# A fused layer norm, attention and SwiGLU kernel: the last reciprocals read out of PSUM ahead of the copies for a flag, and the fallback's DMAs issued by GpSimd

## The chip, the cores and the metric

The kernel runs on one core of a Trainium2 chip. The metric is the device time of one execution in microseconds (us). Where a profile is quoted, its *span* is the time from the first to the last instruction of that execution; the device time is 1.8 to 2.0 us longer in most runs.

## The reference

```python
xn = layernorm(x)                           # x: 1 x 2048 x 512, bf16
s  = attention(xn, wq, wk, wv) @ wo         # 32 heads of 16; one k and one v head for all
g  = silu((silu(xn @ w_gate) * (xn @ w_up)) @ w_down)
return x + s * g
```

## The kernel before

A scheduler in the kernel lays some 20,000 instructions on the engines for the first 764 us. It takes the softmax without subtracting a maximum. That is right as long as the denominators are in range, so at the end a flag is computed from them; if it is raised, a fallback recomputes everything exactly. For the inputs here it is not raised, and every engine jumps over the fallback. The change touches the end of the kernel alone:

```python
    def tq_norm(half, qqs, src):          # src: transposed outputs in PSUM, denominators among them
        ...
        return [nc.vector.tensor_copy(out=dl[:, half, q0:q1, :, :], in_=t4[:, :, :, d0:d0 + 1]),
                nc.vector.reciprocal(out=rd[:, half, q0:q1, :, :], in_=dl[:, half, q0:q1, :, :]),
                nc.vector.tensor_tensor(out=o_tok[...], in0=t4[:, :, :, v0:v0 + DH], in1=rd[...], op=ALU.mult)]
    ...
    tq01, tq23 = ring[lb][:, 0:512], o_ps[:]
    tp = [ring[la][:, 512:1024], ring[lb][:, 512:1024]]
    ...
    for h, src in ((0, tq01), (1, tq23)):
        qqs = (2 * h, 2 * h + 1)
        tadd("DVE", tq_norm(1, qqs, src))
        tb = tp[h].bitcast(BF16)
        tadd("PE", [nc.tensor.transpose(out=tb[:, k * P:(k + 1) * P], in_=o_tok[:, qq, :], identity=ident_bf[:])
                    for k, qq in enumerate(qqs)])
        tadd("ACT", nc.scalar.copy(out=oTl[:, NQ - 1, h * H2:(h + 1) * H2], in_=tb[:, 0:2 * P]))
    dlf = dl[:].rearrange("p h q g o -> p (h q g o)")
    tadd("DVE", nc.vector.tensor_scalar(out=dlc[:], in0=dlf, scalar1=DEN_LO, scalar2=DEN_HI, op0=ALU.max, op1=ALU.min))
    ...                                    # three more small operations: all in range? -> fmin
    ...                                    # last projection matmuls; flag matmul between tiles 1 and 2
    tadd("DVE", e_out_mul(LN, obk[0], dsts[0]))
    ...                                    # flag_i; its loads on all engines; multiplies and adds of four tiles
    for k in range(4):
        tadd("SP", e_out_st(LN + k))       # the four last stores, 128 KB each
    MAIN.close()
    with tc.If(flag > 0):
        _exact_max_path(...)               # the fallback; its DMAs are issued by nc.sync
```

`tadd` keeps the order on each engine.

## Time and profile before

| | before |
|---|---|
| device time, 4 runs | median 780.86 us, 780.45 to 781.15 |
| span of the profiled run | 778.8 us |
| busy: TensorE, VectorE, ScalarE | 96%, 94%, 97% |
| VectorE's last add (L695) ends | 773.44 us |
| last store: end of issue, 15th of its 16 parts landed, 16th | 774.18, 775.65, 776.07 us |
| SyncE: end of its branch, next instruction | 774.27, 776.87 us |

The busy shares tell about the first 764 us, the rows below about the end, where the change is. The landings are the trace's updates of the store's semaphore: sixteen for one store. The prediction shows the lines of the profile that these readings rest on.

### The profile page before, as it was taken

What the parts mean: (1) busy time and instruction counts of PE and PEld (TensorE: products, weight loads), DVE (VectorE), ACT (ScalarE), POOL (GpSimd) and SP (SyncE); (2) the same over time, 40 slices, a digit from 0 to 9 for tenths busy, and PEclk for the clock granted to TensorE, in tenths of its full rate; (3) what the DMA queues carried; (4) which work ended last, traced back from release to release, by engine and by line L of the source; (5) the groups of instructions that cost most, each with busy time, mean ns of one, the idle gap of its engine ahead of it and who ended that gap; (6) DMA issues with size and microseconds to landing.
All of it is one profiled execution on the core that took longest, in us unless ns stands there. A gap on an engine that the chain in (4) does not pass through costs nothing.

```text
span 778.8 us, 20698 instructions
## 1 busy us (share of the span) xinstructions
PE 748.9 (96%) x9093; PEld 229.7 (29%) x9095; DVE 734.0 (94%) x920; ACT 756.9 (97%) x866; POOL 54.2 (7%) x59
## 2 busy tenths in 40 slices
PE   8999999999999999999999999999999999999995
PEld 3323223322222333322233322322223233322221
DVE  7689999999999999999999999999999999999995
ACT  6999999999999999999999999999999999999993
POOL 2100000000012000000001110000000300000101
PEclk9999999999999999999999999999999999999998
DMA  9400000000001000000000100000000000000001
GB/s 327 141 9 9 16 2 24 3 8 17 4 28 50 23 2 6 18 2 24 2 10 22 49 24 2 24 1 9 16 2 24 28 23 2 2 23 3 22 2 32
DMA packets 21193, 20.15 MB, mean 26 GB/s; under 512 B 8744, under 2 KB 17192, under 8 KB 21096
## 3 DMA queue, kind: packets, MB, share of 16 engines
q1 hardware_dynamic: 19512, 18.20, 7.7%
q8 instruction: 73, 1.20, 0.6%
q10 hardware_dynamic: 1584, 0.56, 0.3%
q14 instruction: 24, 0.20, 0.1%
HBM read 14.19 MB, written 2.34 MB: 21 GB/s over the span
## 4 chain that ended last, share of the span: by engine, by line
PE 48%; ACT 45%; DVE 5%; issue 1%; SPq 0%; DMA 0%; ACTq 0%; POOL 0%; DVEq 0%; POOLq 0%
ACT Pb L937 41%; PE ring L877 17%; PE m_ps L488 16%; PE o_ps L747 13%; ACT th L657 3%; DVE Bf L997 1%; ACT g_sb L937 1%; PE ring L433 1%; DVE Bf L1016 1%; ACT th L674 1%; DVE x_sb L997 0%; DVE Bf L1023 0%; PE ring L488 0%; DVE x_sb L1016 0%; PE ring L452 0%
## 5 line engine op out<-in xcount | busy, mean ns | idle before, releaser
L937 ACT ACTIVATE Pb<-ring 128x1024 bf16<-128x1024 f32 x772 | 730.7, 1202 | 2.1 <-PE ring L877 2.1
L877 PE MATMUL ring<-QB,KT 32*128 32x512 bf16 x2048 | 306.0, 382 | 15.6 <-ACT Pb L937 9.3
L997 DVE TENSOR_SCALAR Bf<-ring 128x1024 uint16<-128x1024 f32 x172 | 209.2, 1216 | 5.2 <-PE ring L877 3.7
L877 PEld LDWEIGHTS <-KT 32*128 32x128 bf16 x2048 | 94.1, 90 | 313.9 <-issue 307.4
L747 PE MATMUL o_ps<-Pb,VA 128*32 128x512 bf16 x1544 | 146.9, 385 | 0.0
L997 DVE TENSOR_SCALAR x_sb<-ring 128x1024 uint16<-128x1024 f32 x72 | 87.6, 1217 | 2.7 <-PE ring L877 2.4
L1016 DVE TENSOR_TENSOR Bf<-Bf,Bf 128x2048 f16<-128x2048 f16 x74 | 90.0, 1216 | 0.1
L747 PE MATMUL o_ps<-xnT,zw 128*32 128x512 bf16 x1092 | 83.1, 381 | 0.0
L488 PE MATMUL m_ps<-xnT,wu_sb 128*32 128x512 bf16 x896 | 72.6, 384 | 1.1 <-DVE ab L659 1.1
L488 PE MATMUL m_ps<-wd_sb,hT 128*32 128x512 bf16 x896 | 71.5, 383 | 0.1
L488 PE MATMUL m_ps<-xnT,wg_sb 128*32 128x512 bf16 x896 | 70.4, 384 | 0.0
L747 PE MATMUL o_ps<-Bf,VD 128*32 128x512 f16 x688 | 67.1, 385 | 0.4 <-DVE Bf L1016 0.3
L732 POOL TENSOR_TENSOR oT<-oa,rb 128x512 bf16<-128x512 f32 x15 | 22.7, 1514 | 614.2 <-DMA rb<-dscr 515.7
L1023 DVE TENSOR_SCALAR Bf<-Bf 128x2048 uint16<-128x2048 uint16 x86 | 60.4, 702 | 0.6
L747 PEld LDWEIGHTS <-VA 128*32 128x32 bf16 x1560 | 38.0, 94 | 53.8 <-issue 51.5
L1011 DVE TENSOR_SCALAR Bf<-Bf 128x2048 uint16<-128x2048 uint16 x74 | 52.1, 712 | 0.0
L657 ACT ACTIVATE th<-m_ps 128x512 f32<-128x512 f32 x56 | 43.7, 781 | 0.0
L659 DVE SCALAR_TENSOR_TENSOR ab<-th,m_ps 128x512 f32<-128x512 f32 x56 | 38.1, 680 | 4.2 <-ACT th L657 3.9
L663 DVE TENSOR_TENSOR hT<-ab,m_ps 128x512 bf16<-128x512 f32 x56 | 38.1, 680 | 2.1 <-PE m_ps L488 1.7
L747 PEld LDWEIGHTS <-VD 128*32 128x32 f16 x976 | 26.6, 94 | 38.9 <-issue 35.3
L747 PEld LDWEIGHTS <-zw 128*32 128x32 bf16 x1092 | 25.8, 95 | 25.5 <-issue 12.9
L1016 DVE TENSOR_TENSOR x_sb<-x_sb 128x2048 f16<-128x2048 f16 x24 | 29.2, 1215 | 0.0
(121 smaller groups left out, 414.3 us busy)
## 6 DMA issues: line engine op xcount, KB each, us to landing
rb<-dscr SPq DMA_DIRECT2D x15, 256.0 KB
out_dram<-xn SPq DMA_DIRECT2D x16, 128.0 KB, 1.9
dn<-oa SPq DMA_DIRECT2D x120, 2.0 KB, 1.7
oa<-oa SPq DMA_DIRECT2D x60, 32.0 KB, 2.0
wg_sb<-in_B_w_gate_dram SPq DMA_DIRECT2D x1, 1792.0 KB, 12.3
wu_sb<-in_B_w_up_dram SPq DMA_DIRECT2D x1, 1792.0 KB
wd_sb<-in_B_w_down_dram SPq DMA_DIRECT2D x1, 1792.0 KB, 19.7
x_sb<-in_A_x_dram SPq DMA_DIRECT2D x3, 512.0 KB
```

Source lines behind the costliest of these rows:

```text
L488: return [nc.tensor.matmul(out=dst[GRP * j:GRP * j + GRP, :], lhsT=w[:, GRP * j:GRP * j + GRP], rhs=rhs, start=start, stop=stop, tile_posi ...
L657: t_ = OP("ACT", 0.477, [a], lambda: nc.scalar.activation(out=th[i][:], in_=m_ps[:], func=ACT.Tanh, scale=0.5), (0,), name="tanh")
L659: s_ = OP("DVE", 0.6, [t_, ab_rel[i]], lambda: nc.vector.scalar_tensor_tensor(out=ab[i][:], in0=th[i][:], scalar=1.0, in1=m_ps[:], op0=ALU ...
L663: h = OP("DVE", 0.6, [b], lambda: nc.vector.tensor_tensor(out=hT[:, f, :], in0=ab[i][:], in1=m_ps[:], op=ALU.mult), (1,), name="hmul")
L732: return [pk, q], lambda eng: eng.tensor_tensor(out=oT[qs % 2][:, jj, :], in0=o0[:], in1=rbt[:], op=ALU.mult)
L747: r.append(nc.tensor.matmul(out=o_ps[GRP * g:GRP * g + GRP, :], lhsT=lhs, rhs=rhs, start=(n == 0), stop=(n == pv_total[(b, g)] - 1), tile_ ...
L877: return lambda: [nc.tensor.matmul(out=ring[sl][:, u * 512:(u + 1) * 512], lhsT=KT[half][GRP * g:GRP * g + GRP, t * P:(t + 1) * P], rhs=QB ...
L937: bi = nc.scalar.activation(out=buf, in_=ring[i][:], func=ACT.Exp, scale=escale, bias=ebias)
L997: lambda: nc.vector.tensor_scalar(out=U[:, hs], in0=ring[si][:], scalar1=ubias, scalar2=UINF, op0=ALU.add, op1=ALU.min), (1.5, u), name="p ...
L1011: o1 = OP("DVE", 0.6, [pa, pa0] + wrel, lambda: nc.vector.tensor_scalar(out=Bf[wi], in0=U, scalar1=0x3FF, scalar2=0x3800, op0=ALU.bitwise_and,
L1016: return lambda: eng.tensor_tensor(out=Bf[wi][:, a:z].bitcast(FP16), in0=Bf[wi][:, a:z].bitcast(FP16), in1=U[:, a:z].bitcast(FP16), op=ALU ...
L1023: o2 = OP("DVE", 0.6, o3, lambda: nc.vector.tensor_scalar(out=U, in0=U, scalar1=0x7C00, scalar2=None, op0=ALU.bitwise_and), (2, u, 1), nam ...
```

## The change

Its intent is twofold. The reciprocals of the last block's denominators need not wait for the copy that the flag needs, so they read PSUM directly and the copies come later. And SyncE, which issues the last stores and then jumps over the fallback's DMAs, should have nothing to jump over: GpSimd, idle by then, issues those DMAs.

```diff
@@ fallback
-                        nc.sync.dma_start(out=MR[row:row + 1, :], in_=tms[r0:r0 + NT, :])
+                        nc.gpsimd.dma_start(out=MR[row:row + 1, :], in_=tms[r0:r0 + NT, :])
-            nc.sync.dma_start(out=xr[:], in_=x_v[:, n, :])
+            nc.gpsimd.dma_start(out=xr[:], in_=x_v[:, n, :])
-            nc.sync.dma_start(out=out_v[:, n, :], in_=res[:])
+            nc.gpsimd.dma_start(out=out_v[:, n, :], in_=res[:])
@@ tq_norm
-        return [nc.vector.tensor_copy(out=dl[:, half, q0:q1, :, :], in_=t4[:, :, :, d0:d0 + 1]),
-                nc.vector.reciprocal(out=rd[:, half, q0:q1, :, :], in_=dl[:, half, q0:q1, :, :]),
+        return [nc.vector.reciprocal(out=rd[:, half, q0:q1, :, :], in_=t4[:, :, :, d0:d0 + 1]),
+    def tq_den(half, qqs, src):
...
+        return nc.vector.tensor_copy(out=dl[:, half, q0:q1, :, :], in_=t4[:, :, :, d0:d0 + 1])
@@ g_h0 (half 0)
-        ... lambda: tq_norm(0, range(4), m_ps[:]) ...
+        ... lambda: tq_norm(0, range(4), m_ps[:]) + [tq_den(0, range(4), m_ps[:])] ...
@@ tail, behind the loop over h
         tadd("ACT", nc.scalar.copy(out=oTl[:, NQ - 1, h * H2:(h + 1) * H2], in_=tb[:, 0:2 * P]))
+    for h, src in ((0, tq01), (1, tq23)):
+        tadd("DVE", tq_den(1, (2 * h, 2 * h + 1), src))
     dlf = dl[:].rearrange("p h q g o -> p (h q g o)")
```

More of the change, by code (lines that the diff above doesn't have):

```diff
@@ L1064, in tq_norm @@
                     in1=rd[:, half, q0:q1, :, :].to_broadcast([P, q1 - q0, 4, DH]), op=ALU.mult)]
+    def tq_den(half, qqs, src):
+        q0, q1 = qqs[0], qqs[-1] + 1
+        t4 = src[:, 0:(q1 - q0) * P].rearrange("p (q g c) -> p q g c", g=4, c=GRP)
+        d0 = DH * (1 - half)
+        return nc.vector.tensor_copy(out=dl[:, half, q0:q1, :, :], in_=t4[:, :, :, d0:d0 + 1])
     def g_h0():
@@ L1070, in g_h0 @@
                    (2,), "f", "fill")
-        m_rel[0] = OP("DVE", 0.8, [a], lambda: tq_norm(0, range(4), m_ps[:]), (1,), name="h0")
+        m_rel[0] = OP("DVE", 0.8, [a], lambda: tq_norm(0, range(4), m_ps[:]) + [tq_den(0, range(4), m_ps[:])], (1,), name="h0")
     def g_checks():
```

## The prediction

> **What bounds the kernel now.** The page first. Three engines are busy nearly all of the 778.8 us, and the chain of work that ended last alternates between them:
>
> ```profile
> PE 748.9 (96%) x9093; PEld 229.7 (29%) x9095; DVE 734.0 (94%) x920; ACT 756.9 (97%) x866; POOL 54.2 (7%) x59
> ...
> PE 48%; ACT 45%; DVE 5%; issue 1%; SPq 0%; DMA 0%; ACTq 0%; POOL 0%; DVEq 0%; POOLq 0%
> ```
>
> So nothing off these engines counts in the first 764 us. The change leaves that stretch as it is: placing the two built programs side by side, the order of instructions on TensorE, ScalarE and VectorE differs only in line numbers, in one early place (half 0 of the last block, at 750.8 us, where copy, reciprocal, multiply become reciprocal, multiply, copy) and in the tail. I therefore read the tail. This is VectorE's timeline there (start, duration, line, operation):
>
> ```profile
> 767.02 0.17 DVE L1059 COPY dl<-ring 128x8 f32<-128x8 f32 x1 [0.33 <-PE ring L1051]
> 767.23 0.20 DVE L1060 RECIPROCAL rd<-dl 128x8 f32<-128x8 f32 x1
> 767.46 0.29 DVE L1061 TENSOR_TENSOR o_tok<-ring,rd 128x128 bf16<-128x128 f32 x1
> 767.67 0.15 DVE L1059 COPY dl<-o_ps 128x8 f32<-128x8 f32 x1
> 767.86 0.20 DVE L1060 RECIPROCAL rd<-dl 128x8 f32<-128x8 f32 x1
> 768.10 0.29 DVE L1061 TENSOR_TENSOR o_tok<-o_ps,rd 128x128 bf16<-128x128 f32 x1
> 768.31 0.17 DVE L1344 TENSOR_SCALAR dlc<-dl 128x32 f32<-128x32 f32 x1
> ...
> 768.96 0.16 DVE L1347 TENSOR_REDUCE fmin<-fmin 128x1 f32<-128x3 f32 x1
> ```
>
> and the end of the same view:
>
> ```profile
> 769.33 0.69 DVE L690 SCALAR_TENSOR_TENSOR ab<-ring,g_sb 128x512 f32<-128x512 f32 x1 [0.22 <-PE ring L488]
> ...
> 772.50 0.93 DVE L695 TENSOR_TENSOR xn<-oa,x_sb 128x512 bf16<-128x512 f32 x1
> ```
>
> From 769.33 to 773.43 VectorE has no gap, so whatever moves its L690 forward moves the last L695, and with it the last output store. What L690 waits for is TensorE's L488, itself behind ScalarE's L1342, the transposes L1340 and VectorE's L1061.
>
> The chain of work ends at 773.43, but the span goes on to 778.8. These 5.4 us are queue instructions, which the chain leaves out. The waits of the SyncE queue from 764 us on show the largest of them, and the branch's line (L1376) shows whose it is (duration in ns, first and last start):
>
> ```profile
> SPq L1376 <- SPq L1376: 2.6, 1, 2.6
> ```
> ```profile
> L1376 SPq EVENT_SEMAPHORE  x8: 17/17/17, 776.9 to 777.4; - x8
> L1376 ACTq COMPARE_BRANCH  x1: 50/50/50, 770.6 to 770.6; - x1
> ...
> L1376 POOLq COMPARE_BRANCH  x1: 45/45/45, 771.9 to 771.9; - x1
> L1376 DVEq COMPARE_BRANCH  x1: 72/72/72, 772.5 to 772.5; - x1
> L1376 ACTq EVENT_SEMAPHORE  x1: 17/17/17, 773.5 to 773.5; - x1
> L1376 SPq COMPARE_BRANCH  x1: 45/45/45, 774.2 to 774.2; - x1
> ...
> L1376 DVEq EVENT_SEMAPHORE  x1: 21/21/21, 775.4 to 775.4; - x1
> ```
>
> An engine that has code in the fallback jumps over it and then stands still: ScalarE 770.6 to 773.5, VectorE 772.5 to 775.4, SyncE 774.2 to 776.9. GpSimd has none there, and by the trace its next instruction starts 0.12 us after its branch (771.93 to 772.05). SyncE is last to branch, since it issues the last store before (773.81 to 774.18). Is its 2.6 us only the landing of that store? By the trace's semaphore updates 15 of its 16 parts have landed by 775.65 and the last at 776.07. SyncE wakes at 776.87, so the jump itself costs 0.8 us beyond the landing. Then it does eight semaphore additions (776.87 to 777.46, 0.60 us), nine closing waits and the barrier of all engines, to 778.80.
>
> [...]the trace [...]gives 2.6 to 2.9 us (2.60, 2.82 and 2.78 from branch end to next instruction on SyncE, ScalarE and VectorE). [...]L1061 to the PSUM copy L1059 is 0.21 us, L1061 to L1344 out of SBUF is 0.21 us too. [...]
>
> **Part 1, reciprocals from PSUM.** The copy goes from ahead of each reciprocal to behind both multiplies. First half: L1061 starts one copy step sooner, 767.23 - 767.02 = 0.21 us. Second half: also without its own step (767.86 - 767.67 = 0.19), together 0.40 us. Followed on: transposes of half one at 767.60 instead of 767.81, where TensorE is just through with its dummy matmuls (it sat idle 0.20 us before L1340); ScalarE's first L1342 at 767.98 instead of 768.19, its second at about 768.36 instead of 768.77, now waiting for ScalarE itself; L488 for tiles 0 and 1 at 768.45; so L690 can start at 769.12. VectorE must also be free. It still has the same ten small operations, now with the two copies next to each other and independent of one another: multiply at 767.70, copies at 767.91 and about 768.0, the four flag operations from about 768.2 to 769.0. That is about 0.1 us before 769.12, so L690 is set by TensorE, and the flag matmul, which stands ahead of tiles 2 and 3 on TensorE, comes no later either. Gain 0.21 us, on the path up to the last store[...]. The early place at 750.8 us has the same three operations in all, m_ps is released after the same work, and the sum there is zero.
>
> **Part 2, fallback's DMAs on GpSimd.** In the built program the fallback has 186 instructions of SyncE before; after, SyncE has one (a branch) and GpSimd has the 186. So:
> - SyncE no longer jumps over code: the 2.60 us go, as GpSimd's 0.12 us shows. What stays is the landing. Last landing 776.07 - 0.21 = 775.86, against 776.87: 0.8 us from here, beside the 0.21.
> - The eight semaphore additions leave SyncE: 0.60 us, also behind the landing, so a full gain.
> - Four closing waits are added ahead, for the semaphores of GpSimd's DMAs, 0.065 us each by the spacing of the present closing waits. They are done before the landing and cost nothing, if GpSimd has added to these semaphores by then.
> - GpSimd now makes the jump: branch at 771.88 - 0.21 = 771.67, next instruction 2.6 to 2.9 us later, 774.3 to 774.6, four waits at 0.08, then one instruction that adds to all eight. Its other form takes 27 ns at the start of this trace; this form is nowhere in it[...]. [...]
>
> Now the end: SyncE's wait for the last store is the second of the closing waits with a transfer. Before it started at 777.53, and 1.27 us later the span was over. After: 775.86 + 0.05 + 1.27 = 777.18, plus some 0.05 for clearing 25 semaphores instead of 17 (135 ns for 17): 777.2. Gain of the span 1.6 us: 0.2 from part 1, 1.4 from part 2 (0.8 of stall, 0.6 of additions). The timed median is 781.01, so 779.4. That is 0.2%.
>
> **Rivals.**
> 1. GpSimd takes SyncE's place. If the fetch takes as long as TensorE's (3.6 us in its branch) and the adding instruction 1 us or more, GpSimd is done at 771.72 + 3.6 + 0.3 + 1 = 776.6; SyncE then has the rest of the closing waits still ahead, and the end is near 778.0: gain 0.8, time 780.2. For it: the instruction is not in the trace. Against: three of four jumps took under 2.9 us.
> 2. The landing comes sooner. One part of the last store landed 0.42 us after all others, while instruction fetches of 8 to 16 KB each ran[...] (one of 16 KB took 1.16 us from 775.19). Were that SyncE's own fetch, it falls away: end near 776.8, time 779.0.
> 3. The stall is no fetch but all landing, so part 2 gives only the 0.6 us: gain 0.8, time 780.2. Against it: ScalarE stands as long with no transfer to wait for.
> 4. Part 1 is eaten: the reciprocal out of PSUM is slower, or VectorE's flag operations come later. Gain 1.4, time 779.6.
> 5. A slower main body, from moved code or a changed rhythm at 750.8 us. The orders are the same; I give it little.
>
> **Range and chances.** The three runs before spread over 0.7 us, half the expected gain, and the size of rivals 1 and 2 is 0.4 to 0.8 us. Range 778.6 to 780.2. 2% would be 15.6 us, three times the whole stretch behind 773.4, so faster or slower by that much is left at 1% each at most.
>
> **What would show it.** In the profile after: VectorE's last L695 ending 0.15 to 0.25 us sooner, with two reciprocals from ring and o_ps ahead of both copies (right for part 1). SyncE's first instruction behind its branch within 0.2 us of it, no eight additions there, GpSimd's gap of 2.6 us or more behind its own branch, and SyncE's last long wait ending on a store's semaphore (right for part 2) or on one of GpSimd's (rival 1). A span under 777.0 speaks for rival 2. I am wrong if SyncE still stands 2.6 us, if the stretch behind the last L695 stays at 5.4 us, or if that L695 ends no sooner.

The cut marks stand for statements that no trace or run of this case shows, among them an allowance for a slower reciprocal out of PSUM and a guess of the time of GpSimd's adding instruction with the end worked out from it. The forecast's sum: 0.2 us of part 1, 0.8 of the stand-still and 0.6 of the additions make 1.6 us, and 781.01 - 1.6 = 779.4. The "1 us or more" of rival 1 is a supposition; the instruction took 0.175 us in the changed kernel. That the stand-still behind a jump is the wait for an instruction fetch was my reading. What the traces show are stand-stills of 2.60 to 2.82 us (before), with six fetches of 8 KB and two of 16 KB behind the first branch; in e4, which has no jumps, one of 8 KB is left there and none of 16 KB.

## More of the kernel before

`tq01` and `tp[1]` are two halves of one PSUM tile, `ring[lb]`.

## The result, and the profile after

The changed kernel took 781.63 us (median of 4 runs, 779.44 to 781.96) against 780.86 us. The ratio is 1.0004 with a 95% interval of 0.9985 to 1.0023: no change that can be told from none, where 1.4 us less were predicted. Here and below a ratio is the mean time of one kernel's fast runs over that of the other's in the same rounds, so not quite the ratio of the quoted medians. One of the four runs took 779.44 us, which is what was predicted; its span is 777.2 us, the others' are 779.8, 779.8 and 780.1.

VectorE's timeline of the changed kernel (start, duration, line, operation; in brackets the idle time before it and what ended that):

```profile
767.03 0.21 DVE L1059 RECIPROCAL rd<-ring 128x8 f32<-128x8 f32 x1 [0.33 <-PE ring L1051]
767.28 0.29 DVE L1060 TENSOR_TENSOR o_tok<-ring,rd 128x128 bf16<-128x128 f32 x1
767.49 0.20 DVE L1059 RECIPROCAL rd<-o_ps 128x8 f32<-128x8 f32 x1
767.72 0.29 DVE L1060 TENSOR_TENSOR o_tok<-o_ps,rd 128x128 bf16<-128x128 f32 x1
768.79 0.17 DVE L1069 COPY dl<-ring 128x8 f32<-128x8 f32 x1 [0.78 <-ACT oT L1347]
768.87 0.15 DVE L1069 COPY dl<-o_ps 128x8 f32<-128x8 f32 x1
...
769.72 0.16 DVE L1354 TENSOR_REDUCE fmin<-fmin 128x1 f32<-128x3 f32 x1
769.80 0.68 DVE L690 SCALAR_TENSOR_TENSOR ab<-ring,g_sb 128x512 f32<-128x512 f32 x1
...
772.96 0.93 DVE L695 TENSOR_TENSOR xn<-oa,x_sb 128x512 bf16<-128x512 f32 x1
```

The multiplies came as early as predicted (second one at 767.72). But the first copy sat idle for 0.78 us until ScalarE's last copy (L1347) was done, and everything behind it on VectorE moved with it: L690 at 769.80 instead of 769.33, the last L695 ending at 773.89 instead of 773.44. Part 1 cost 0.46 us.

The waits of SyncE's queue from 764 us on (total us, times, longest), changed kernel:

```profile
...
SPq L1411 <- DMA out_dram<-xn: 2.7, 2, 2.3
SPq L698 <- DVE oa L690: 0.7, 1, 0.7
SPq L1411 <- PEq L1411: 0.7, 2, 0.5
...
```

Its own stand-still of 2.6 us is gone from this list. In its place stands a wait for an output store, 2.3 us. The branch's line shows the same and clears GpSimd (duration in ns, first and last start):

```profile
L1383 POOLq EVENT_SEMAPHORE  x4: 17/43/43, 772.8 to 773.1; - x4
...
L1383 POOLq COMPARE_BRANCH  x1: 45/45/45, 772.3 to 772.3; - x1
...
L1383 POOLq INC_SWDGE_SEM  x1: 175/175/175, 773.1 to 773.1; - x1
...
L1383 SPq COMPARE_BRANCH  x1: 50/50/50, 775.0 to 775.0; - x1
```

GpSimd went on 0.44 us behind its branch and had its semaphores added by 773.32, long before anybody needed them. SyncE went on 0.43 us behind its own.

Which store, and why so late? The last one. Fifteen of its parts had landed by 776.50, the sixteenth at 778.43, and the span was over 1.32 us later. Two views of the transfers of the changed kernel show what ran while the sixteenth part was out (queue, kind: packets, MB, share of 16 engines). From 776.0 to 777.25 us:

```profile
q8 instruction: 1, 0.02, 6.4%
q14 instruction: 2, 0.02, 4.5%
q1 hardware_dynamic: 1, 0.00, 0.0%
```

and from 777.25 to 778.5 us:

```profile
DMA packets 9, 0.01 MB, mean 7 GB/s; under 512 B 1, under 2 KB 9, under 8 KB 9
...
q1 hardware_dynamic: 9, 0.01, 3.9%
```

In the first stretch almost nothing moves but instruction fetches, one of them of 16 KB from 776.02 to 777.30. In the second come nine packets of the store: eight rows of 1 KB and the semaphore's 4 bytes, a sixteenth of 128 rows, the first starting at 777.28, 0.015 us before the fetch ends. The trace doesn't say which of the 16 DMA engines did which transfer; that this share stood behind the fetch is my reading of this start, here and below. In the profile of before the last such fetch of 16 KB (775.19 to 776.35) ran beside the share that landed last (packets from 775.29 to 775.65), so that share did not wait for its end.

### The profile page after: what moved, and what is told of

It reads as the page before. It is cut to its first block, busy times and chain, and to the rows that moved or that the text cites. A ratio compares the mean times of both kernels' runs of the same rounds, so it can differ in the third digit from the quotient of the medians.

```text
span 779.8 us, 20701 instructions
## 1 busy us (share of the span) xinstructions
PE 748.3 (96%) x9095; PEld 229.4 (29%) x9095; DVE 734.4 (94%) x920; ACT 757.0 (97%) x866; POOL 52.8 (7%) x59
## 4 chain that ended last, share of the span: by engine, by line
PE 47%; ACT 44%; DVE 6%; issue 1%; POOL 0%; SPq 0%; DMA 0%; ACTq 0%; DVEq 0%; POOLq 0%
ACT Pb L937 39%; PE ring L877 17%; PE m_ps L488 16%; PE o_ps L747 13%; ACT th L657 3%; DVE Bf L997 1%; ACT g_sb L937 1%; DVE Bf L1016 1%; ACT th L674 1%; DVE x_sb L997 0%; DVE Bf L1023 0%; DVE hT L663 0%; DVE Bf L1011 0%; DVE x_sb L1016 0%; PE ring L488 0%
```

## The experiments

Theory A has two halves: (a) the copy out of `ring` waits for ScalarE, since both engines read the tile `ring[lb]`; (b) TensorE's jump over its 16,933 instructions of fallback makes it fetch 16 KB and, when it has gone on, 16 KB more (before: 771.75 to 772.88 and 775.19 to 776.35 us, with its next instruction at 774.40), and one part of the last store waits behind this second fetch. Where an expectation speaks of a page, it is this second fetch. Rivals were a slow reciprocal, GpSimd as the new bound, a store that is slow by itself, and the fetches of the other engines. All kernels gave the right result for these inputs. All had five runs (e10 six) beside the kernel before on the same chip. They used three chips; the kernel before had medians of 781.5, 781.4 and 781.2 us there, in 28 runs, more than in the first four.

This table has from each trace the end of the last store's issue, the landing of its 15th and 16th part, TensorE's second fetch of 16 KB, the span of the traced run, and the spans of all runs:

| kernel | issue ends | 15th | 16th | second fetch | span | all spans |
|---|---|---|---|---|---|---|
| before | 774.18 | 775.65 | 776.07 | 775.19 to 776.35 | 778.8 | 778.3 to 780.7 |
| changed | 774.96 | 776.50 | 778.43 | 776.02 to 777.30 | 779.8 | 777.2 to 780.1 |
| e0 changed, again | 775.60 | 776.96 | 778.27 | 775.96 to 777.13 | 779.6 | 777.6; 779.5 to 779.8 |
| e1 part 1 alone | 774.67 | 776.47 | 778.06 | 775.76 to 776.92 | 779.9 | 778.9; 779.7 to 780.1 |
| e2 part 2 alone | 774.17 | 775.99 | 777.73 | 775.04 to 776.59 | 779.1 | 777.4; 778.7 to 779.1 |
| e3 copies early | 774.18 | 775.63 | 777.37 | 775.17 to 776.23 | 778.7 | 778.6 to 778.9 |
| e11 e3 again | 774.79 | 776.23 | 778.01 | 775.90 to 776.86 | 779.3 | 777.0; 778.7 to 779.6 |
| e10 e3, SyncE | 774.24 | 776.10 | 777.72 | 775.27 to 776.58 | 779.6 | 779.3 to 780.2 |
| e4 e3, no fallback | 773.50 | 774.84 | 774.88 | none | 776.5 | 776.4 to 776.5 |
| e6 e3, none on TensorE | 773.48 | 775.21 | 775.35 | none | 776.7 | 776.7 to 777.5 |
| e5 e3, TensorE later | 774.28 | 775.71 | 775.95 | 776.06 to 777.08 | 777.3 | 777.0 to 778.0 |
| e9 e5 again | 774.99 | 776.36 | 776.38 | 776.67 to 777.63 | 777.7 | 777.3 to 777.7 |
| e8 e3, TensorE half as late | 775.41 | 776.78 | 778.04 | 776.62 to 778.08 | 779.4 | 776.9 to 779.4 |
| e7 before, TensorE later | 775.30 | 776.77 | 776.97 | 777.60 to 778.56 | 780.2 | 778.6 to 780.2 |

### e0: the changed kernel again

> The changed kernel once more, for the spread of its runs. Theory A (part 1 costs 0.46 us because the copy of the denominators waits for ScalarE's last copy; part 2 takes SyncE's stand-still away, but in most runs one of the 16 parts of the last store waits 2 us behind TensorE's 16 KB instruction fetch): two groups of runs, most near 781.6, some near 779.4, in all five rounds; in the profile L695 ends near 773.9 and the last landing is either under 776.7 or over 778. Rival B (the 779.4 was a chance low, and landings are always late): one group near 781.6. Rival C (the late landing was the chance): most near 779.8.

Measured: 781.50 us, ratio 0.9997 (0.9983 to 1.0011). Four spans at 779.5 to 779.8, one at 777.6. Two groups, as theory A has it; the trace fell into the upper one, with the 16th part 1.3 us late. L695 ended at 774.19, where the whole tail began 0.3 us later; from the first reciprocal to L690 it took 2.77 us again.

### e1: part 1 alone

The edit puts `nc.gpsimd` of the three fallback lines back to `nc.sync`.

> Part 1 without part 2: reciprocals from PSUM, copies behind, the fallback's DMAs back on SyncE. Theory A: VectorE's last L695 ends at 773.9 (0.46 later than before) and SyncE again stands 2.6 us behind its branch, so the span is 779.3 and the time 781.4 to 781.5; if the last part of the store lands as late as in the changed kernel's trace, 782. Rival D (part 1 gains 0.2 us as predicted, and something of part 2 delays the copies): L695 ends at 773.2, time 780.7.

Measured: 781.83 us, ratio 1.0001 (0.9988 to 1.0015). From the first operation on the denominators to L690: 2.77 us, as in the changed kernel; before it was 2.31 (767.03 to 769.33). So the loss is part 1's own; rival D is out. L695 ended at 773.75, the whole tail lying 0.14 us earlier than in the changed kernel. SyncE's waits:

```profile
SPq L1383 <- SPq L1383: 3.3, 2, 2.6
```

That is the stand-still of 2.59 us, after which SyncE waits a second time, 0.7 us, for the late part. With the fallback on SyncE, too, a late part is there, and the span is then 779.9, as expected for that case.

### e2: part 2 alone

The edit is the three fallback lines alone.

> Part 2 without part 1: the old order on VectorE, the fallback's DMAs on GpSimd. Theory A: L695 ends at 773.44 as before, SyncE goes on within 0.5 us of its branch; if the last store lands at 776.1 as before, the span is 777.5 and the time 779.5; in runs where one part falls behind TensorE's fetch, 781 to 781.5. Rival E (GpSimd's queue or its semaphores delay the end): the end comes a fixed time behind GpSimd's addition, not behind the landing.

Measured: 780.87 us, ratio 0.9989 (0.9976 to 1.0003). L690 came 2.31 us behind the first copy, as before. SyncE went on 0.44 us behind its branch at 774.26, then waited until 777.75 for the late part; the end came 1.31 us behind that. Rival E is out: GpSimd was done at 772.82. One run of five had the short span, 777.4; the others were late, as the second half of the expectation had it.

### e3: the copies written earlier

```diff
         tadd("DVE", tq_norm(1, qqs, src))
+        if h == 1:
+            tadd("DVE", [tq_den(1, (0, 1), tq01), tq_den(1, (2, 3), tq23)])
         tb = tp[h].bitcast(BF16)
...
-    for h, src in ((0, tq01), (1, tq23)):
-        tadd("DVE", tq_den(1, (2 * h, 2 * h + 1), src))
```

> The changed kernel with the two copies written ahead of the last transposes and of ScalarE's last copy, so that VectorE does not wait for ScalarE. Theory A: copies at 767.9 and 768.0, L690 at 769.1 instead of 769.8, last L695 ending at 773.2, flag matmul and stores 0.65 us sooner than in the changed kernel; span 777.2 where the last store lands cleanly (time 779.2 to 779.4), near 779 where a part lands late (time 781). Rival F (the copies were late for another reason, a slow reciprocal out of PSUM or the order of VectorE's queue): copies still at 768.8 or the gain under 0.3 us.

Measured: 780.61 us, ratio 0.999 (0.9976 to 1.0003). VectorE's timeline:

```profile
766.87 0.21 DVE L1059 RECIPROCAL rd<-ring 128x8 f32<-128x8 f32 x1 [0.33 <-PE ring L1051]
...
767.55 0.29 DVE L1060 TENSOR_TENSOR o_tok<-o_ps,rd 128x128 bf16<-128x128 f32 x1
767.76 0.16 DVE L1069 COPY dl<-ring 128x8 f32<-128x8 f32 x1
767.83 0.16 DVE L1069 COPY dl<-o_ps 128x8 f32<-128x8 f32 x1
...
768.93 0.69 DVE L690 SCALAR_TENSOR_TENSOR ab<-ring,g_sb 128x512 f32<-128x512 f32 x1
```

No idle time before the copies, and L690 2.06 us behind the first reciprocal: 0.70 us better than the changed kernel and 0.24 better than before. The built programs say why. In the changed kernel and in this one, VectorE's order is the same; only the place in the kernel's text differs, and with it the wait:

```
changed:  L1069 TensorCopy dl<-ring_97 128x8 [waits Activation_49]
e3:       L1069 TensorCopy dl<-ring_97 128x8
```

So here the build ordered the two engines' reads of one PSUM tile as the text has them, though they read different halves of it: with the copies behind, VectorE idled 0.78 us for ScalarE, with them ahead not at all. Half (a) is shown, and rival F is out. The same order now costs a little elsewhere: TensorE's second pair of transposes writes the other half of that tile, and in e3's trace it waited 0.23 us for the copies. The time gained only 0.26 us on e2; in the trace SyncE waited 2.0 us for the store, until 777.38, and the five spans, all within 0.3 us, give no sign of a run without the late part.

### e4: no fallback at all

```diff
-    with tc.If(flag > 0):
+    if False:
         _exact_max_path(...)
```

> The kernel with the early copies, and the whole fallback and its branch taken out (flag still computed and loaded; right for these inputs, wrong where the flag would be raised). [...]Theory A (a late 16th part of the last store comes from TensorE's 16 KB instruction fetches behind its jump): no instruction fetches behind 771 us, all 16 parts of the last store within 0.4 us of each other, about 1.3 us behind the end of its issue, and the end 1.3 us behind that: span 776.3, time 778.2, in all runs alike. Rival G (one part of a store is slow by itself, for instance by memory): the 16th part is still 1 to 2 us late, span near 778.5, time 780.3.

Measured: 778.34 us, ratio 0.9961 (0.9948 to 0.9975), spans 776.4 to 776.5 in all five. The issue of the stores and their landing (duration in ns; us), and SyncE's wait for them:

```profile
L698 SPq DMA_DIRECT2D out_dram<-xn x16: 332/338/579, 232.0 to 773.2; - x16
...
DMA to landing us min/median/max: 1.7/1.7/2.1
```
```profile
SPq L1411 <- DMA out_dram<-xn: 1.3, 2, 0.8
```

One fetch of 8 KB, at 775.9 us and so behind the landings, was left, where none was expected. Without jumps the 16 parts land within 0.18 us of each other, and no run differs by more than 0.14 us from another. Rival G, a part that is slow by itself, is out. Beside e3's 780.61 and e11's 781.15 us, on two other chips, the jumps cost 2.3 to 2.8 us. The late part is not all of it. From L695's end to the last landing it took 4.33 us in e3 and 1.74 in e4: the 16th part lags 1.74 us behind the 15th instead of 0.04, and the last issue ends 1.15 us behind L695 instead of 0.36. In e3 the issue of the second store took 1.25 us while TensorE's first fetch ran, and the stores behind it came later.

### e6: a fallback without TensorE

The fallback is a stub of 2300 VectorE, 2000 ScalarE and 135 GpSimd instructions, so the kernel would be wrong where the flag is raised.

> The kernel with the early copies, with a fallback of about as many instructions on VectorE, ScalarE and GpSimd but none on TensorE (it would give a wrong result where the flag is raised; it is not here). VectorE and ScalarE still jump and fetch in pieces of 8 KB, TensorE does not. Theory A: no 16 KB fetch behind 771 us, the 16th part of the last store within 0.5 us of the others, span 776.9 to 777.1, time 778.9. Rival H (the 8 KB fetches delay it): late part at about 777.4 as in the kernel with the early copies, span 778.7, time 780.6.

Measured: 779.04 us, ratio 0.997 (0.9956 to 0.9983). Transfers from 764 us on in this kernel, in the same columns as above:

```profile
q14 instruction: 6, 0.05, 0.7%
q8 instruction: 1, 0.02, 0.2%
```

The changed kernel has six and three there. The two fetches of 16 KB that are gone were therefore TensorE's (the one left lies ahead of the jump), and the 8 KB ones are the other engines'. With these six still there, the 16th part is 0.13 us behind the 15th. Rival H is out as the cause of the late part in e3: in all five runs the span stays at 777.5 or less. But the spans scatter over 0.8 us, more than in e4, so what is left of the jumps may not be free either; and e8 below has a late part that started as an 8 KB fetch ended, within 0.003 us.

### e5 and e9: TensorE's branch 1.1 us later

```diff
-    tadd("DVE", e_out_mul(LN + 2, obk[2], dsts[2]))
+    mul2 = e_out_mul(LN + 2, obk[2], dsts[2])
+    tadd("DVE", mul2)
+    for l in loads:
+        if l.ins.engine == nc.tensor.engine:
+            tc.add_manual_dep(l.ins, mul2.ins.name, <synchronised>, reason="later branch on PE")
```

> The kernel with the early copies, where TensorE's load of the flag (and so its branch) waits for VectorE's third multiply, about 1.1 us later. Theory A: the page[...] starts at about 776.0 instead of 775.2, behind the last store: the 16th part lands by 775.7, span 777.0, time 778.9. Its first fetch falls on the earlier stores, whose late part has time. Rival G: the late part stays, span 778.7, time 780.6. Rival H (the fetches of the other engines do it): as G.

> The kernel with the 1.1 us once more, on the same chip as the one above: spans 777.0 to 778.0 again, time 779.9; below the kernel before by 1 to 1.5 us.

Measured: e5 779.94 us, ratio 0.9986 (0.9973 to 1.0000); e9 780.77 us, ratio 0.9993 (0.998 to 1.0007). The second fetch starts behind the store, and the 16th part is 0.24 and 0.02 us behind the 15th, in place of 1.7: theory A's central point. The edit moves both of TensorE's fetches, though, so it does not leave everything else as it was. The span came out as expected. The time did not, and it did not repeat well, for two reasons. The first fetch now falls on the last store's issue:

```profile
L698 SPq DMA_DIRECT2D out_dram<-xn x16: 332/346/1378, 231.8 to 772.9; - x16
```

1.38 us at 772.90 (1.87 in e9), where e4 takes 0.33. And the device time is 2.6 to 3.4 us more than the span in these ten runs, where it is 1.8 to 1.9 in e4 and e6. In the two traces the span ends 0.19 and 0.08 us behind TensorE's second fetch; whether that is why is not shown. The short runs of the changed kernel, e0 and e2 have it too (2.2, 2.5 and 2.8 us), and four of e8 (2.3 to 2.9), the one short run of e11 has not (1.9). No record covers that time; what it is stays open. So a span and a device time can't be taken for each other in this kernel.

### e8: half as late

The same edit on `e_out_mul(LN + 1, ...)`.

> The kernel with the early copies, TensorE's load of the flag held back by VectorE's second multiply instead of the third, about 0.5 us instead of 1.1 us later than without. If what counts is only that the page[...] starts behind the last store: first fetch at about 771.9 to 773.0, in time to leave the issue of the last store alone (in the run with 1.1 us it took 1.38 us), the second at about 775.5, just behind the store's parts at 775: span 776.8 to 777.2, time 778.9. If the second fetch still meets the last store: 778.5, time 780.4, in some or all rounds.

Measured: 780.32 us, ratio 0.9984 (0.997 to 0.9998), spans from 776.9 to 779.4. A mixture: in the trace, the first fetch (772.16 to 774.46) held the third store's issue for 2.20 us, so the fourth ran into the later fetches after all. Here the late share did not wait for the 16 KB fetch (776.62 to 778.08): its first packet starts at 776.906, as an 8 KB fetch of another engine ends (776.602 to 776.909), and it lands at 778.04, before the 16 KB one is over. So in this trace the part started with the end of a small fetch; what fits theory A in all eight late traces is the start at the end of an instruction fetch, and TensorE's is the one in the seven others. In each of these the late share's first packet starts 0.014 to 0.015 us before that fetch ends.

### e7: the kernel before, TensorE later

> The kernel before, with TensorE's load of the flag held back in the same way, by 1.1 us. The kernel before shows two groups of spans, 778.7 to 778.8 and 779.5 to 780.1. Theory A: the upper group are runs with the late part, and SyncE's stand-still up to 776.9 hides all of an early one; with TensorE later only the lower group is left, time 780.6 in all five rounds. Rival I (the two groups come from the first 764 us, for instance the clock): both groups stay.

Measured: 781.21 us, ratio 0.9996 (0.9982 to 1.0009), spans 778.6 to 780.2. The expectation failed: the upper runs did not go. The trace shows why it is no test of the late part. There is none (776.97), but the first fetch (773.08 to 775.01) held the last issue for 1.78 us, so SyncE branched at 775.34 instead of 774.22 and then stood still to 778.26. What makes the kernel before scatter over 2.4 us in 28 runs is therefore not shown. e1 and e10 have its arrangement on SyncE, and in both traces the part is late; its own single trace is one without. That its upper runs are those with a late part is likely, but not shown.

### e10 and e11: the mended part 1 without and with part 2

e10 is e3 with the fallback's DMAs on SyncE, e11 is e3 again.

> Part 1 mended (early copies) without part 2 (the fallback's DMAs on SyncE). From first denominator operation to the first multiply with the gate about 2.06 us as in the kernel with the early copies (before 2.31, changed kernel 2.76), so the last store is issued as early. SyncE stands 2.6 us behind its branch, and in runs with a late 16th part waits for that with seven of its eight additions still to do, so 0.5 us behind the kernel with the early copies: time 781.1, spans 779.1 to 779.4, or 778.4 where the part is not late. If part 2 brings nothing even then: 780.6, as the kernel below.

> The kernel with the early copies again, beside the one above on the same chip: spans 778.6 to 778.9 with the late part as on the first chip, time 780.6; if some rounds have no late part, spans near 777.0.

Measured on one chip: e10 781.56 us, ratio 1.0005 (0.9992 to 1.0017); e11 781.15 us, ratio 0.9991 (0.9977 to 1.0005). L690 came 2.06 us behind the first reciprocal in both. In e10 SyncE awoke at 777.01 and waited on for the part that landed at 777.72; from that to the end it took 1.86 us, in e11 1.32. So of part 2 only the additions that are left out (0.53 us) reach the end when the part is late: the stand-still is hidden behind it. e11 did not repeat e3's narrow spans; one of its five runs was short.

## Why the prediction was wrong

The steps in their order, with the profiled run of the changed kernel. Predicted was a span of 777.2, measured 779.76.

- **Part 1, the step "copies at 767.91", and with it "L690 is set by TensorE": wrong.** The gain on the multiplies was right, 0.38 us on the second where 0.40 was predicted, and so was the chain behind it: where the copies do not wait (e3, e10, e11), L690 gains 0.24 us on before, 0.21 predicted. What failed is that the copies, moved behind ScalarE's last copy in the text, took on a wait for it. The last L695 ended 0.46 later instead of 0.21 earlier: **0.67 us** of the miss. I had compared the orders of the two programs, not the waits at each instruction, which show it.
- **Part 2, the step "Last landing 776.07 - 0.21 = 775.86": wrong.** It took the 2.63 us from L695's end to the last landing in one trace for a constant. It was 4.54 us: **1.91 us** of the miss, of which 1.52 are the 16th part's lag behind the 15th (1.94 instead of 0.42) and 0.33 the later end of the last issue. The trace taken was also one of the better ones: its span was 778.8, and 7 of the 28 later runs of the kernel before had 778.9 or less. Rival 2 had named the instruction fetches that ran beside the store, but as something that would fall away; and it took the fetch at 775.19 for possibly SyncE's. It is TensorE's (e6), and stays.
- **SyncE's stand-still and its additions go: right**; SyncE goes on 0.43 us behind the branch (I had said within 0.2), with no additions. 1.32 us from landing to end, 1.37 predicted (-0.05). But a late part hides the 0.8 us expected from the stand-still.
- The three terms, 0.67 + 1.91 - 0.05 = 2.53, make the 777.2 into 779.7.
- **Rival 1, GpSimd takes SyncE's place: did not happen.** I gave its jump 2.6 to 2.9 us, it took 0.44.
- **The reciprocal out of PSUM, counted without extra time: right.** It starts 0.24 us before its multiply, as the one out of SBUF did (767.226 to 767.463 before, 767.034 to 767.278 after).
- **The early place at 750.8 us is worth nothing, and the body does not change: in line with it.** In the two traces the first denominator operation of the tail starts at 767.03 both times.
- **The range** rested on three runs before that spread over 0.7 us. The later 28 spread over 2.4 us; a range of 1.6 us was too narrow for either.

The 779.44 us run with its span of 777.2 is no proof of the sum, since part 1's loss was in it too; it has no trace.

None of the complete versions is clear of the kernel before by 2%; the best, e5 and e8, are at 0.9986 and 0.9984, and e9 did not confirm the first.

## What to carry to other kernels

When an instruction moves in the text, compare the waits that the build gives it, not only its place in the order: here VectorE's read of a PSUM tile took on a wait of 0.78 us for ScalarE's read of the same tile. At a kernel's end, list what else is transferred while the last store is under way: here TensorE's jump over 16,933 instructions came with two fetches of 16 KB (neither is there in e4 and e6), the second when the jump was already over, 0.7 to 1.5 us behind TensorE's next instruction. Removing a wait gained only down to the next landing here (in e2 SyncE went on 0.44 us behind its branch, then waited for the landing until 777.75), so take that landing from more than one trace.

## What the runs show of jumps, fetches and stores

- The runs with the real fallback show 2.4 to 3.2 us from the branch's end to the next instruction on ScalarE, VectorE and (where it has the DMAs) SyncE, and a branch of 3.5 to 4.8 us on TensorE. Behind the jumps, fetches of 16 KB are seen on TensorE's queue alone, and the other engines' come as transfers of 8 KB (e6: the two of 16 KB are gone, the six of 8 KB are there).
- SyncE went on 2.60 us behind its branch over 186 skipped instructions (before), GpSimd 0.44 us over the same 186 (changed kernel) and 1.01 us over 135 (e6). What makes the difference is not shown.
- A part of a store landed 1.14 us behind the end of a 16 KB fetch in seven of eight traces with a late part (1.136 to 1.144 us), up to 1.9 us behind the other fifteen. The issue of a store of 128 KB took 1.2 to 2.2 us instead of 0.33 in all twelve traces with TensorE's first fetch; it ended 0.30 to 0.48 us behind that fetch. A fetch of 16 KB stands in these traces as one transfer of 0.9 to 2.3 us, and in those seven the store's share starts as it ends, 0.014 to 0.015 us before.
- For the reciprocal of 128 x 8 elements no difference was seen: 209 and 195 ns out of PSUM, 203 ns out of SBUF.
